# Q of all batches transposed by DMA, an opening ordered along its longest path, and split folds in a fused sorted-attention, Fourier-mix and MLP kernel

## The chip, the cores and the metric

The kernel runs on one core of one Trainium2 chip. The metric is the device time in microseconds (us), start to end. Executions of one kernel scatter here by about 2%, so small differences are judged only from ratios of fast runs of the same rounds, with their 95% intervals. A run is called slow when it took over 1.5% longer than the fastest run of the same kernel.

Five engines work side by side: TensorE multiplies matrices, VectorE and ScalarE work through their elements, GpSimd does small operations and issues loads, and SyncE issues transfers only. Each issues its transfers in order, as a queue; all queues are carried by 16 DMA engines. A transfer has landed when its completion is signalled. A point is one per cent of the time of the kernel before.

## The reference

Inputs are q, k, v (4 batches, 8 heads, 768 rows, 64 columns), a sorting matrix per batch and head, and two MLP weights. Cut to what matters:

```python
P = sort_net                                  # five Sinkhorn steps on 8x8 matrices
for _ in range(5):
    P = exp(P - max); P = P / rowsum; P = P / colsum
k_sorted = einsum('bhij,bhjcd->bhicd', P, k_blocks)      # v_sorted likewise
attn = softmax(q_blocks @ k_sorted_blocks^T / 8) @ v_sorted_blocks
x = attn, heads side by side                             # (4, 768, 512)
u = x + real(fft(fft(x, axis=1), axis=2))
un = (u - mean(u)) / sqrt(var(u) + 1e-6)
out = u + relu(un @ w_ch1) @ w_ch2                       # w: 512x2048, 2048x512
```

## The kernel before

The program makes its own schedule. Every operation is an object with a cost per engine, what it reads and writes, and a priority; a list scheduler written in Python puts the operations in order on each engine. Hardware then runs each engine's list strictly in order.

Q must stand with the head dimension on partitions before the scores. For batches 2 and 3 (`QB`) the DMA transposes it; for 0 and 1 a copy regroups it, TensorE transposes it, and another copy brings it back.

```python
QB = (2, 3)
def load_qk(nm, b, hf, prio):
    src = {"k": k, "q": q}[nm]
    if nm == "q" and b in QB:                 # natural layout: one load per head, 128-byte runs
        for h in range(4):
            load(kq[:, slot[nm, b, hf], :].rearrange(...)[:, h // 2, h % 2], src[b, 4 * hf + h]..., ...)
        return
    load(kq[:, slot[nm, b, hf], :]..., ...)   # one large load of four heads
# in kqt(b, hp):
if b in QB:
    P.add({"SP": (1.4, 3.4)}, lambda _: nc.sync.dma_start_transpose(qt.ap..., kq[:, slot["q", b, hf], 768 * hl:768 * hl + 768]), ...)
    return
for r in range(6):
    nc.tensor.matmul(p16[:, 128 * r:128 * r + 128], qr.ap[:, r], idh, is_transpose=True)
# ... copied back to qt by ScalarE or VectorE
```

The weights w1 and w2, K, Q and V are loaded from GpSimd's queue. The sync queue carries the DMA transposes and, for each batch, three small copies that put the rows of the Fourier mix's correction in place (`rb<-rr`).

```python
for dst, src in ((rb[0:32, :], rr[o:o + 32, 0, :]), (rb[32:64, :], ...), (rb[64:96, :], ...)):
    P.add({"SP": (0.1, 2.3)}, lambda _, dst=dst, src=src: nc.sync.dma_start(dst, src), ...)
# dft1: two adds over all 512 columns fold the six row blocks
for n in range(2):
    V.tensor_tensor(pmt[:, 3 * n:3 * n + 3, 0:DM], rt.ap[:, 0:3, :], rt.ap[:, 3:6, :], op=add if n == 0 else subtract)
```

The softmax here doesn't subtract the row's maximum and nothing guards it: scores larger than these inputs give would overflow.

## Time and profile before

| | before |
|---|---|
| time, median of 3 runs (range) | 299.42 us (298.74 to 299.74) |
| the profiled run | 300.78 us, a slow run |
| its first product with w1, the first layer of the MLP | 76.06 us |
| w1 / w2 / V of batch 1 in flight (counted from the trace's DMA records) | 30.6–41.6 / 40.4–51.9 / 50.6–59.2 us |

Lines of the page and the views stand in the prediction. Three habits help to read them. A digit row is the span in 40 slices of 7.5 us, each digit the busy tenths. A busy TensorE is not a full one, so work is counted as matmuls times their closest spacing. And an average over the span hides the regimes: this kernel loses nearly all its time before the first normalised rows reach the MLP.

The only profile of the kernel before is of a slow run, and the prediction reads it without saying so. A fast one of nearly the same program came later: z2 below (295.71 us) has the same order of instructions on TensorE, VectorE, ScalarE and GpSimd, and one unread DMA transpose more. Its first w1 product comes at 72.6 us. Most of the difference arises early: in the slow profile the trace's first record of TensorE's full clock starts at 36.0 us, in z2's at 23.6 us. (The page's clock row shows 9s before that as well, where it has no record.) The mix of batch 0's V, first in the slow profile, then in z2 (duration in ns, first and last start in us):

```profile
L638 PE MATMUL bank<-bdv,vbn x64: 219/219/311, 30.6 to 40.2; 128*128 128x128 f16 x63, 128*96 128x128 f16 x1
L638 PE MATMUL bank<-bdv,vbn x64: 217/219/219, 29.1 to 36.1; 128*128 128x128 f16 x63, 128*96 128x128 f16 x1
```

Where an opening is compared below, z2 stands for the kernel before.

### The profile page before, as it was taken

What the parts mean: (1) busy time and instruction counts of PE and PEld (TensorE: products, weight loads), DVE (VectorE), ACT (ScalarE), POOL (GpSimd) and SP (SyncE); (2) the same over time, 40 slices, a digit from 0 to 9 for tenths busy, and PEclk for the clock granted to TensorE, in tenths of its full rate; (3) what the DMA queues carried; (4) which work ended last, traced back from release to release, by engine and by line L of the source; (5) the groups of instructions that cost most, each with busy time, mean ns of one, the idle gap of its engine ahead of it and who ended that gap; (6) DMA issues with size and microseconds to landing.
All of it is one profiled execution on the core that took longest, in us unless ns stands there. A gap on an engine that the chain in (4) does not pass through costs nothing.

```text
span 299.0 us, 5829 instructions
## 1 busy us (share of the span) xinstructions
PE 271.8 (91%) x2332; PEld 166.4 (56%) x2332; DVE 178.3 (60%) x395; ACT 153.3 (51%) x307; POOL 55.1 (18%) x91
## 2 busy tenths in 40 slices
PE   0499988884999999899999999999999999999994
PEld 0266976763556656555556645545645645645641
DVE  4797589999699999786249954314605315312001
ACT  2575579862647797468237703613721631641710
POOL 8964212012800036030002000200200010010000
PEclk9999999996699999999999999999999999999999
DMA  7999999980920249825010210031021121121002
GB/s 116 218 286 216 216 206 213 203 111 15 67 17 2 58 98 162 150 13 107 35 71 15 55 70 35 20 105 38 15 53 70 37 53 70 37 54 70 37 0 105
DMA packets 43025, 26.32 MB, mean 88 GB/s; under 512 B 29834, under 2 KB 38552, under 8 KB 42996
## 3 DMA queue, kind: packets, MB, share of 16 engines
q0 software_dynamic: 22576, 15.16, 33.3%
q1 hardware_dynamic: 20422, 10.78, 12.4%
q8 instruction: 18, 0.29, 0.4%
q14 instruction: 9, 0.07, 0.1%
HBM read 28.95 MB, written 6.29 MB: 118 GB/s over the span
## 4 chain that ended last, share of the span: by engine, by line
PE 72%; DVE 16%; DMA 4%; ACT 2%; issue 2%; POOL 2%; DVEq 0%; ACTq 0%; POOLq 0%
PE bank L1112 28%; PE bank L1091 25%; PE bank L635 3%; DVE rt L905 2%; DMA kq<-in_q_dram 2%; PE bank L1005 2%; PE bank L952 2%; PE bank L851 2%; PE bank L891 2%; DMA out_dram<-u 2%; PE bank L638 2%; DVE pmt L919 2%; PE bank L797 2%; DVE u L1020 1%; PE bank L1012 1%
## 5 line engine op out<-in xcount | busy, mean ns | idle before, releaser
L1103 ACT ACTIVATE hr<-bank 128x384 f16<-128x384 f32 x111 | 54.1, 490 | 79.9 <-PE bank L1091 79.7
L1091 PE MATMUL bank<-ut,w1sb 128*128 128x384 f16 x512 | 93.4, 331 | 0.7 <-DVE hr L1100 0.7
L1112 PE MATMUL bank<-w2sb,hr 128*128 128x512 f16 x384 | 89.0, 379 | 0.0
L1091 PEld LDWEIGHTS <-w1sb 128*128 128x128 f16 x512 | 49.5, 99 | 36.1 <-issue 3.0
L1112 PEld LDWEIGHTS <-hr 128*128 128x128 f16 x384 | 36.5, 98 | 40.6 <-issue 0.2
L1120 DVE TENSOR_TENSOR u<-bank,u 128x512 f32<-128x512 f32 x24 | 16.6, 690 | 51.5 <-PE bank L1112 51.0
L1020 DVE SCALAR_TENSOR_TENSOR u<-rt,bank 128x512 f32<-128x512 f16 x24 | 16.1, 678 | 35.6 <-PE bank L1012 29.7
L860 ACT ACTIVATE ex<-bank 96x384 f32<-96x384 f32 x64 | 27.9, 485 | 8.3 <-PE bank L851 6.5
L1033 POOL TENSOR_SCALAR mv<-mv 128x3 f32<-128x3 f32 x8 | 2.6, 320 | 141.8 <-DVE mv L1028 139.6
L1052 ACT ACTIVATE un<-u,nm,ny 128x512 f16<-128x512 f32 x14 | 11.4, 811 | 14.6 <-POOL nm L1042 9.0
L395 POOL DMA_DIRECT2D kq<-in_q_dram x20 | 17.7, 905 | 4.2 <-ACT qr L571 1.9
L891 PE MATMUL bank<-vsf,eb 97*128 97x65 f16 x384 | 15.8, 195 | 2.7 <-DVE u L1020 1.3
L905 DVE TENSOR_TENSOR rt<-bank,rz 128x384 f16<-128x384 f32 x32 | 17.3, 550 | 0.4
L874 ACT ACTIVATE eb<-ex,negone 96x384 f16<-96x384 f32 x29 | 17.5, 614 | 0.2
L891 PEld LDWEIGHTS <-eb 97*128 97x128 f16 x384 | 14.3, 98 | 4.8 <-issue 2.9
L571 ACT CAST vsf<-bank 96x512 f16<-96x512 f32 x19 | 13.9, 790 | 4.3 <-PE bank L638 3.4
L1026 DVE BATCH_NORM_STATS2 st<-u 128x6 f32<-128x512 f32 x24 | 15.9, 682 | 0.2
L395 POOL DMA_DIRECT2D kq<-in_k_dram x8 | 6.5, 808 | 49.9 <-issue 27.8
L826 PE MATMUL bank<-pack,qr 128*128 128x128 f16 x48 | 5.3, 264 | 11.0 <-ACT qr L571 10.2
L635 PE MATMUL bank<-bdv,vcx 128*128 128x128 f16 (+1 forms) x128 | 14.2, 238 | 1.1 <-ACT bdv L571 1.1
L872 DVE TENSOR_SCALAR eb<-ex 96x384 f16<-96x384 f32 x35 | 13.1, 377 | 1.7 <-ACT ex L860 1.6
L797 PE MATMUL bank<-bdk,kq 128*64 128x128 f16 x192 | 11.8, 247 | 1.5 <-DVE u L1020 1.0
(114 smaller groups left out, 337.8 us busy)
## 6 DMA issues: line engine op xcount, KB each, us to landing
out_dram<-u SPq DMA_DIRECT2D x24, 256.0 KB, 2.0
kq<-in_k_dram POOLq DMA_DIRECT2D x8, 384.0 KB, 9.2
w1sb<-in_moe_w_ch_dram POOLq DMA_DIRECT2D x4, 512.0 KB, 15.2
w2sb<-in_moe_w_ch_dram POOLq DMA_DIRECT2D x4, 512.0 KB, 19.0
kq<-in_q_dram POOLq DMA_DIRECT2D x4, 384.0 KB, 11.3
hr<-in_v_dram POOLq DMA_DIRECT2D x2, 768.0 KB, 11.5
kq<-in_v_dram POOLq DMA_DIRECT2D x2, 768.0 KB, 21.3
kq<-in_q_dram POOLq DMA_DIRECT2D x16, 96.0 KB, 6.0
```

Of the source, the lines that this page charges most:

```text
L395: return P.add({eng: c}, lambda _: e.dma_start(dst, src), r=r, w=w, prio=prio, nbytes=nbytes, tag="load", after=after)
L635: nc.tensor.matmul(o, vcx[:, 96 * d:96 * d + m], bd, start=True, stop=(t == 1))
L797: nc.tensor.matmul(ps.ap[64 * h2:64 * h2 + 64, 128 * r3:128 * r3 + 128], k16[:, 2 * hl + h2, 3 * half + r3, :], bdk[:, 2 * hp + h2].rearra ...
L860: nc.scalar.activation(ex.ap, pss[h2].ap[0:96, 0:384], AF.Exp, scale=SCALE),
L874: nc.scalar.activation(ed, src, AF.Identity, bias=negone[0:96])
L891: nc.tensor.matmul(po.ap[:, 65 * T:65 * T + 65], eb.ap[:, e0:e0 + 128], vsf[:, vi:vi + 65], start=(n == 0), stop=(n == 1), skip_group_chec ...
L905: P.add({"DVE": (0.45, 0.56)}, lambda _: V.tensor_tensor(rt.ap[:, :, D * h:D * h + D], po3()[:, :, 0:D], rz.ap[:, :, None].broadcast_to([1 ...
L1020: V.scalar_tensor_tensor(u.ap.rearrange("p (m n) -> p m n", n=2), rt.ap[:, T, :].rearrange("p (m n) -> p m n", n=2), RSC, ps.ap.rearrange( ...
L1091: nc.tensor.matmul(ps.ap[:, 0:GT], w1sb[:, c, 128 * fc:128 * fc + 128], ut.ap[:, c, :], start=(c == 0), stop=(c == 3))
L1103: nc.scalar.activation(hr[g][:, fc, :], ps.ap[:, 0:GT], AF.Relu)
L1112: nc.tensor.matmul(ps.ap, hr[g][:, fc, 128 * tt:128 * tt + 128], w2sb[:, fc, :], start=(fc == 0), stop=(fc == 15))
L1120: V.tensor_tensor(u.ap, ps.ap, u.ap, op=ALU.add),
```

## The change

Its intent is to shorten that opening: take the Q transposes and their copies off TensorE, ScalarE and VectorE, and let the scheduler follow the longest path to the first normalised rows. The diff, cut to its core (left out: bookkeeping of tiles, other scratch buffers for the correction rows, and two constants of the scheduler's model of loads):

```diff
-QB = (2, 3)
+LOOK = {"DVE": 0.8, "ACT": 0.8, "PE": 0.8}
+QB = (0, 1, 2, 3)
...
+    def aim(self, goal):                # priority = length of the longest path to the goal
+        tail = {goal: 0.0}
+        for o in reversed(self.ops):
+            if o in tail:
+                for p in o.preds:
+                    tail[p] = max(tail.get(p, 0.0), tail[o] + best(o))
+        for o, t in tail.items():
+            o.crit = True
+            if o.nbytes == 0:
+                o.prio = -1000.0 - t
...
+                        if not o.crit and e in LOOK:   # don't start an operation off the path if one on
+                            ...                        # the path gets ready within 0.8 of its cost
...
-    many("qr", 2, [128, 6, 128], F16)
-    many("qt", 3, [128, S], F16)
+    many("qt", 5, [128, S], F16)
...
-        for n in range(2):
-            P.add({"DVE": (0.86, 0.95)}, ...tensor_tensor(pmt[:, 3 * n:3 * n + 3, 0:DM], ...
+        for c in range(2):
+            for n in range(2):
+                cc = slice(256 * c, 256 * c + 256)
+                P.add({"DVE": (0.44, 0.55)}, ...tensor_tensor(pmt[:, 3 * n:3 * n + 3, cc], ...
...
-            if b > 0:
+            if b + g > 0:               # second row group of batch 0 by DMA transpose too
...
-    at(-30.0, (dft1, (0,)), (dft2, (0, 0)), (dft2, (0, 1)))
+    at(-30.0, (dft1, (0,)))
+    goal.append(dft2(0, 0))
+    at(-29.0, (dft2, (0, 1)))
```

More of the change, by code (lines that the diff above doesn't have):

```diff
@@ L101 @@
     __slots__ = ("n", "costs", "fn", "preds", "succs", "left", "ready", "prio",
-                 "vts", "fresh", "nbytes", "end", "start", "eng", "tag")
+                 "vts", "fresh", "nbytes", "end", "start", "eng", "tag",
+                 "crit")
 class Buf:
@@ L116 @@
 class Plan:
-    HBM = 330.0
+    HBM = 400.0
     DLAT = 2.2
@@ L134, in add @@
         o.n = len(self.ops)
+        o.crit = False
+        o.end = o.start = None
         o.costs, o.fn, o.nbytes, o.tag = costs, fn, nbytes, tag
@@ L166, in add, with best @@
         return o
+    def aim(self, goal):
+        def best(o):
+            return min(c[1] for c in o.costs.values()) + self.XL
+        tail = {goal: 0.0}
[7 more added lines that the diff above has]
+                o.prio = -1000.0 - t
     def schedule(self):
@@ L202, in slot_time, with soonest @@
             return (None if short else t), short
+        crits = [o for o in self.ops if o.crit]
+        def soonest(c, e):
+            if e not in c.costs:
+                return None
+            for p in c.preds:
+                if p.start is None:
+                    if p.left or len(p.costs) > 1:
+                        return None
+                    x, = p.costs
+                    return max(free[x], p.ready[x]) + p.costs[x][1] + self.XL
+            return None
         while todo:
             pick = None
+            want = {}
+            near = [c for c in crits if c.start is None and c.left == 1]
+            for e in free:
+                for o in avail[e]:
+                    if o.fresh and o.ready[e] <= free[e] + 0.3:
+                        for p in slot_time(o, ())[1]:
+                            want[p] = min(want.get(p, o.prio), o.prio)
             for e in free:
@@ L209, in schedule @@
                 soon = None
-                held = set()
                 for o in sorted(avail[e], key=lambda o: (o.prio, o.n)):
@@ L213, in schedule @@
                     if o.fresh:
-                        st, short = slot_time(o, held)
-                        if o.ready[e] <= t + 0.3:
-                            held |= short
+                        st, short = slot_time(
+                            o, [p for p in want if want[p] < o.prio])
                         if st is None:
@@ L220, in schedule @@
                     if s <= t + 1e-9:
+                        if not o.crit and e in LOOK:
+                            x = t + LOOK[e] * o.costs[e][0]
+                            n = [c.ready[e] for c in avail[e] if c.crit
+                                 and t < c.ready[e] < x]
+                            n += [y for y in (soonest(c, e) for c in near)
+                                  if y is not None and t < y < x]
+                            if n:
+                                n = min(n)
+                                if soon is None or n < soon:
+                                    soon = n
+                                continue
                         cand = o
@@ L408, in qk16, with kqk @@
             "p (h r d) -> p h r d", h=4, r=6)
+    def kqk(n):
+        return [("kq", n, h) for h in range(4)]
     def load_qk(nm, b, hf, prio):
@@ L417, in load_qk @@
                     src[b, 4 * hf + h].rearrange("(r p) d -> p r d", r=6),
-                    196608, [("kq", slot[nm, b, hf])], prio + 0.01 * h)
+                    260000, [("kq", slot[nm, b, hf], h)], prio + 0.01 * h)
             return
@@ L422, in load_qk @@
                  "h (p r) d -> p h (r d)", r=6), 786432,
-             [("kq", slot[nm, b, hf])], prio)
+             kqk(slot[nm, b, hf]), prio)
     def hk(g):
@@ L432, in load_v @@
             [("nat", t, hf)] + (hk(0)[8 * hf:8 * hf + 8] if t == 0 else
-                                [("kq", 2 * hf), ("kq", 2 * hf + 1)]), prio)
+                                kqk(2 * hf) + kqk(2 * hf + 1)), prio)
     def load_w1(c, prio):
@@ L476 @@
     for n, nm in enumerate(("pw", "pack", "vrow", "erow", "rrow")):
-        load_c(nm, -500.0 + n, "SP")
-    load_qk("k", 0, 0, -500.0)
-    load_qk("q", 0, 0, -499.0)
-    load_v(0, 0, -498.0)
-    load_v(0, 1, -497.0)
-    load_qk("k", 0, 1, -496.0)
-    load_qk("q", 0, 1, -495.0)
-    load_c("dtab", -494.0)
-    load_c("lt", -493.0)
+        load_c(nm, -5000.0 + n, "SP")
+    load_qk("k", 0, 0, -5000.0)
+    load_qk("q", 0, 0, -4999.0)
+    load_v(0, 0, -4998.0)
+    load_v(0, 1, -4997.0)
+    load_qk("k", 0, 1, -4996.0)
+    load_qk("q", 0, 1, -4995.0)
+    load_c("dtab", -4994.0)
+    load_c("lt", -4993.0)
     load_c("cs", 19.0)
@@ L581, in v_path @@
         psm = Buf("pm", "pf") if t else Buf("pm")
-        stage = [("kq", n) for n in range(4)] if t else hk(0)
+        stage = [i for n in range(4) for i in kqk(n)] if t else hk(0)
         for hf in range(2):
@@ L673, in a_path @@
         pa = Buf("pf")
-        bd_, bp_ = Buf("qt"), Buf("qt")
+        bd_, bp_ = Buf("un"), Buf("un")
         P.add(pe(0.4), lambda _: nc.tensor.matmul(
@@ L709, in a_path @@
         px, pr = Buf("pf"), Buf("pf")
-        hi, hi2 = Buf("qt"), Buf("qt")
+        hi, hi2 = Buf("yr"), Buf("ex")
         def f(_):
@@ L731, in a_path @@
               r=[pr], w=[hi], tag="rhi")
-        P.add(evac(512), lambda e: copy(e, hi2.ap[0:64, 0:512],
+        P.add(evac(512), lambda e: copy(e, hi2.ap[0:64, 0:256].bitcast(F16),
                                         px.ap[0:64]),
@@ L748, in a_path @@
             rr[0:64, 1, :].rearrange("p (n m) -> p n m", n=2),
-            hi2.ap[0:64, 0:512].rearrange("p (m n) -> p n m", n=2),
+            hi2.ap[0:64, 0:256].bitcast(F16).rearrange(
+                "p (m n) -> p n m", n=2),
             nlo[0:64], px.ap[0:64].rearrange("p (m n) -> p n m", n=2),
@@ L755, in a_rows @@
         o = 32 * (b % 2)
-        for dst, src in ((rb[0:32, :], rr[o:o + 32, 0, :]),
-                         (rb[32:64, :], rr[64 + o:96 + o, 0, :]),
-                         (rb[64:96, :], rr[o:o + 32, 1, :])):
+        for n, (dst, src) in enumerate((
+                (rb[0:32, :], rr[o:o + 32, 0, :]),
+                (rb[32:64, :], rr[64 + o:96 + o, 0, :]),
+                (rb[64:96, :], rr[o:o + 32, 1, :]))):
             P.add({"SP": (0.1, 2.3)}, lambda _, dst=dst, src=src:
                   nc.sync.dma_start(dst, src),
-                  r=[("rr", i) for i in (0, 1, 2, 3, 256)], w=["rb"],
+                  r=[("rr", i) for i in (0, 1, 2, 3, 256)], w=[("rb", n)],
                   tag="arow")
@@ L782, in q_copy @@
             e, qr.ap.rearrange("p r (h d) -> p r h d", h=2), src),
-            r=[("kq", slot["q", b, hf])], w=[qr], tag="qcp",
+            r=kqk(slot["q", b, hf])[2 * hl:2 * hl + 2], w=[qr], tag="qcp",
             after=[exps[-1]] if first else [])
@@ L801, in f @@
                             bdk[:, 2 * hp + h2].rearrange("p i c -> p (i c)"))
-            P.add(pe(0.22), f, r=[("kq", slot["k", b, hf]),
+            P.add(pe(0.22), f, r=kqk(slot["k", b, hf]) + [
                                   ("bdk", hp // 2)],
@@ L817, in kqt @@
                 kq[:, slot["q", b, hf], 768 * hl:768 * hl + 768]),
-                r=[("kq", slot["q", b, hf])], w=[qt], tag="qX")
+                r=kqk(slot["q", b, hf])[2 * hl:2 * hl + 2], w=[qt],
+                tag="qX")
             return
@@ L896, in av @@
         P.add(pe(0.5), f, r=[(eb, 0), (eb, 1), "erow", "vrow", "vsz"]
-              + [("vsb", n) for n in range(16)], w=[po], tag="av")
+              + [("vsb", n) for n in range(16)], w=[po, (rts[b], "a", h)],
+              tag="av")
         rz = Buf("rz")
@@ L917, in dft1 @@
         hs = [(rt, h) for h in range(H)]
-        for n in range(2):
-            P.add({"DVE": (0.86, 0.95)}, lambda _, n=n: V.tensor_tensor(
-                pmt[:, 3 * n:3 * n + 3, 0:DM], rt.ap[:, 0:3, :],
-                rt.ap[:, 3:6, :], op=ALU.add if n == 0 else ALU.subtract),
-                r=hs, w=[("pm", n), ("fq", 0), ("fq", 1)],
-                tag="pmt")
+        for c in range(2):
+            for n in range(2):
+                cc = slice(256 * c, 256 * c + 256)
+                P.add({"DVE": (0.44, 0.55)}, lambda _, n=n, cc=cc:
+                      V.tensor_tensor(
+                          pmt[:, 3 * n:3 * n + 3, cc], rt.ap[:, 0:3, cc],
+                          rt.ap[:, 3:6, cc],
+                          op=ALU.add if n == 0 else ALU.subtract),
+                      r=hs[4 * c:4 * c + 4],
+                      w=[("pm", n, c), ("fq", 0), ("fq", 1)], tag="pmt")
         P.add({"ACT": (0.17, 0.22)},
@@ L926, in dft1 @@
                   pmt[:, :, DM:DM + 1], pmt[:, :, 0:1]),
-              r=[("pm", 0), ("pm", 1)], w=["pm2"], tag="pmc")
-        pms = [("pm", 0), ("pm", 1), "pm2"]
+              r=[("pm", 0, 0), ("pm", 1, 0)], w=["pm2"], tag="pmc")
+        pms = [("pm", n, c) for n in range(2) for c in range(2)] + ["pm2"]
         P.add({"DVE": (0.88, 0.97)}, lambda _: V.tensor_tensor(
@@ L1016, in dft2 @@
                   r=[y4[c][g] for c in range(4)]
-                  + ["rb", "rrow", "lt", "lt96", "lt96a", "lt96b", "dtab"],
+                  + [("rb", n) for n in range(3)] + ["rrow", "lt", "lt96", "lt96a", "lt96b", "dtab"],
                   w=[ps, u], tag="dft2")
@@ L1081, in dft2 @@
                   r=[pt], w=[(ut, tt, 1)], tag="utev")
+        return P.ops[-1]
     def mlp(b, g, pr_pe, pr_v):
@@ L1134, in attn @@
             av(b, h)
+    goal = []
     def at(p, *fns):
@@ L1169 @@
     with tc.manual_schedule():
+        P.aim(goal[0])
         for o in P.schedule():
```

## The prediction

> **What bounds the kernel now.** I read the page first: the busy shares, then the 40 slices.
>
> ```profile
> PE 271.8 (91%) x2332; PEld 166.4 (56%) x2332; DVE 178.3 (60%) x395; ACT 153.3 (51%) x307; POOL 55.1 (18%) x91
> ...
> PE   0499988884999999899999999999999999999994
> ...
> DVE  4797589999699999786249954314605315312001
> ACT  2575579862647797468237703613721631641710
> ...
> PEclk9999999996699999999999999999999999999999
> DMA  7999999980920249825010210031021121121002
> ```
>
> The kernel has two regimes. From slice 11 on TensorE is full and VectorE thins out; before that, VectorE and the DMA queues are the full rows. The 91% hides this, because the end of a matmul is modelled. So I next took the chain that ended last and looked at how far apart matmuls start.
>
> ```profile
> 76.06 3.95 PE bank L1091 x12
> ...
> 101.37 0.86 PE bank L1112 x4
> ...
> 276.19 8.45 PE bank L1091 x52
> 284.64 10.37 PE bank L1112 x48
> ```
>
> Packed, a first-layer matmul (L1091) takes 8.45/52 = 0.1625 us and a second-layer one (L1112) 10.37/48 = 0.216 us. The first twelve take 0.329 us each: half clock. In the same way I took 0.040 us for an attention-times-V matmul, 0.0285 for a score, 0.0445 for a K mix, 0.056 for 128 columns, 0.083 for 193, 0.109 for 256. Count times spacing gives TensorE's real work: 39.5 us before 76.06, 22.8 to 101.3, 30.2 to 134.4, 159.0 to 295.1. The stretches last 76.1, 25.2, 33.1 and 160.7 us, so the time without work is **36.5, 2.4, 2.9 and 1.7 us**. After the last matmul 3.9 us remain. The kernel loses its time in the opening, before the first normalised rows reach the MLP. The view by stretch says who is busy there:
>
> ```profile
> 0.00:76.06 76.06, 54.75 (x703) 42.77 (x704) 62.72 (x161) 47.34 (x91) 30.91 (x52) 0.96 0.97 177
> 76.06:101.20 25.14, 25.08 (x221) 16.27 (x221) 22.59 (x46) 15.42 (x32) 5.45 (x6) 0.91 0.42 35
> ```
>
> The columns are length, then PE, PEld, DVE, ACT, POOL busy, clock, DMA share, GB/s. VectorE is busy 85.3 of 101.2 us. Its 15.9 us of idle time lie mainly before 40 us: waits for the sort matrix, for the V load, for the V mix. From 40 to 70 us it is idle 1.2 us in all. Until about 101 us, when the last ReLU of the first MLP is done and L1112 can start, I therefore count **VectorE** time; after that, TensorE work.
>
> **What the Trainium skill says.** "TensorE: Matmul & The Clock Gate", Part 1, says the array runs at half rate until it has been busy for a window. The trace agrees: 0.329 against 0.1625 us, and a row of 6s in the clock. "DMA: Bandwidth & Descriptors", DMA Transpose (X-bar), restricts the transpose to 2-byte types and to the sync and scalar queues; here it is fp16 on the sync queue, 1.21 us to issue and 2.7 us to land. The same page, Issuing engines are not separate DMA queues, says that all queues share 16 engines; the DMA row (9s up to slice 7) shows there is little room for more in the opening. "Perfetto Trace Analysis", Identifying the Most-Contended Engine, calls matmul busy time a poor measure: 271.8 us busy against 254 us of work here.
>
> **The change, part by part.**
>
> *Q by DMA for batches 0 and 1.* Removed (a group of the page, then the form list of the copy helper's line: count, least/median/most ns, first and last start):
>
> ```profile
> L826 PE MATMUL bank<-pack,qr 128*128 128x128 f16 x48 | 5.3, 264 | 11.0 <-ACT qr L571 10.2 <-DVE rt L905 0.3 <-DVE rr L747 0.3
> L571 ACT COPY qr<-kq x5: 813/825/844, 9.3 to 55.2; 128x768 f16<-128x768 f16 x5
> L571 ACT COPY qt<-bank x5: 798/802/811, 12.0 to 59.3; 128x768 f16<-128x768 f16 x5
> L571 DVE COPY qt<-bank x3: 944/947/958, 11.1 to 45.0; 128x768 f16<-128x768 f16 x3
> L571 DVE COPY qr<-kq x3: 332/347/349, 26.5 to 46.6; 128x768 f16<-128x768 f16 x3
> ```
>
> TensorE: 48 x 0.056 = 2.7 us of work. ScalarE: 5 x 0.825 + 5 x 0.802 = 8.1 us. VectorE: 3 x 0.947 + 3 x 0.347 = 3.9 us. One of those VectorE copies sits at 11.08 us inside the sort iterations and holds the chain for 0.9 us. Added: 8 transposes on the sync queue, and Q loads cut in four:
>
> ```profile
> kq<-in_q_dram POOLq DMA_DIRECT2D x4, 384.0 KB, 11.3
> ...
> kq<-in_q_dram POOLq DMA_DIRECT2D x16, 96.0 KB, 6.0
> ...
> qt<-kq SPq DMA_TRANSPOSE x8, 2.7
> ```
>
> A 96 KB load moves 768 packets of 128 bytes. In the backlog near 118 us about 1,170 such packets start per us, so four take 2.6 us; the one load of 384 KB that they replace takes 1.9 us. Issuing four costs GpSimd 4 x 0.85 = 3.4 us. The four half batches thus put the weight loads back by some 3 us (estimate): w1, landed near 42 us before, lands near 45, long before its use. V lands at most 1 us later.
>
> *Second row group of batch 0 by DMA.* 12 x 0.056 = 0.7 us less on TensorE, and three copies of 0.42 to 0.58 us less. Total TensorE work: 254.4 - 2.7 - 0.7 = 251.0 us.
>
> *Order.* I read the built program's instruction order. The V path now comes before most of batch 0's attention; the first row group is folded and normalised first; only 120 instead of 168 attention-times-V matmuls, 96 instead of 128 scores and 90 instead of 96 K mixes stand before the first L1091. That is 1.9 + 0.9 + 0.3 = 3.1 us of work that moves behind it. Split folds cost nothing much: eight adds of 0.95 us become sixteen of about 0.49 us.
>
> *First MLP start.* Before, the V mix ran from 30.5 to 41 us. Now it can start when V has landed (17.5 us), its sum is done (20.5), reduced (21.5), scaled and masked: 24 to 25 us, ending near 34. VectorE's instructions from there to the third row tile, by their durations, are some 31 us; 34 + 31 plus 1 to 3 us of waits gives the first L1091 at **66 to 68 us** instead of 76.06.
>
> *The end.* The start itself is not the gain, since VectorE must still finish batch 1. I summed all VectorE instructions up to the last ReLU of the first MLP, each with its mean duration: 94.5 us before, 90.6 after. Scaled to the busy time of 85.3 us (instructions overlap a little) that is 3.6 us less. TensorE work still to do at that point: 1.1 us less (3.4 us is removed for good, but in the new order 2.3 us less has been done by then). So the gain is 3.6 + 1.1 = 4.7 us, plus whatever VectorE saves of its 15.9 us of idle time. I count 11.4 us of idle time to the end of the V mix (34 less 22.6 us of work) against 13 before, none lost to half-clock ReLUs at 76 to 80 us, but some for the look-ahead's deliberate waits: about 13.5 us. That saves 2.4 us: gain 7.1 us, total **292.3 us**.
>
> **Rivals.**
> (a) *VectorE is the bound and only its order changes.* If the look-ahead holds VectorE back as much as the new order saves, idle stays at 16 us, and 4.7 us is all: 294.7. For it: between 40 and 70 us VectorE had no idle time to give.
> (b) *The early start pays in full.* If TensorE fills as soon as the MLP starts, 9 us less 3.1 deferred plus 3.4 removed gives 9.3: 290. Against it: between the first L1091 and the last of those ReLUs some 28 us of VectorE work stand beside only 25 us of TensorE work in the new order.
> (c) *The DMA queue takes the place of the removed copies.* If small Q packets and transposes hold V up by 3 us, the whole opening moves: 295 to 296. For it: DMA is at 9 in slices 1 to 7. Against it: V is issued after one half batch of Q, whose data used to stand before it as well.
> (d) *Nothing reaches the end*, as TensorE is full later anyway. Against it: that regime has only 7 us of gaps and simply starts earlier.
>
> **Range and chances.** Between (a), my sum and (b) lie 290 to 295 us. The VectorE idle figure is good to 4 us, the sums to 2. Predicted 292.5, range 288 to 298. The 2% line is at 293.4, just above the prediction: faster 0.55, same 0.43, slower 0.02.
>
> **What would show it.** First L1091 at 64 to 69 us and first L1112 at 93 to 98; TensorE work before the first L1091 near 33 us; VectorE idle up to the first L1112 near 13.5 us; no L571 copies of Q, 16 transposes qt<-kq; w1 landed before 50 us; gaps after the first L1112 still under 6 us. The prediction is wrong if V lands after 19 us, if the first normalised rows wait for a transpose or for GpSimd (its chain now has a 0.8 us load issue inside), or if TensorE shows more than 6 us of gaps between the first L1091 and the first L1112.

## The result, and the profile after

| | before | after |
|---|---|---|
| median of 4 runs of the same rounds (range) | 299.08 us (294.53 to 299.74) | 325.88 us (324.57 to 335.75; the last is a slow run) |
| ratio of fast runs, 95% interval | 1 | 1.0971 (1.0765 to 1.1178) |
| first w1 product / first w2 product | 76.06 / 101.37 us (slow profile; z2: 72.6 / 96.8) | 95.36 / 123.5 us |
| w1 / w2 / V of batch 1 in flight | 30.6–41.6 / 40.4–51.9 / 50.6–59.2 | 41.4–59.3 / 53.4–74.5 / 69.7–81.9 us |
| matmuls | 2332 | 2272 |

A ratio is the mean time of one kernel's fast runs over the mean of the other's fast runs of the same rounds, so it is not quite the ratio of the medians quoted. The changed kernel is 9.7% slower; all runs were correct.

The page of the changed kernel, slices as before:

```profile
PE   0379976001979999987999999999999999999995
...
DVE  5797999000789999977925795431461431431002
...
PEclk9995995655679999998999999999999999999999
DMA  9999999999949200599402020203011203012002
```

A slice is 8.1 us here. TensorE and VectorE now stand still together in the eighth to tenth slice (56 to 80 us), while the DMA engines are full up to the eleventh. Before, no slice of the opening after the first was empty on either engine. From the thirteenth slice on TensorE is as full as it was. The busy times of the opening and of the first MLP stretch, in the columns that the prediction explains:

```profile
0.00:95.36 95.36, 49.24 (x569) 36.42 (x570) 60.20 (x144) 35.38 (x69) 44.99 (x68) 0.77 1.33 160
95.36:123.50 28.14, 27.66 (x335) 18.12 (x336) 27.25 (x67) 25.35 (x56) 0.86 (x1) 0.99 0.37 58
```

In the opening VectorE does slightly less than before (60.20 against 62.72 us) but in 19 us more of time; it is not the bound any more. The second stretch is as dense as its counterpart before. So most of the loss lies before the first w1 product: 22.7 of the 28.9 us between the spans of this profile (322.8 us) and of z2 (293.9 us). The other 6 us lie after it: about 2 us of work that was moved there, and TensorE's time without work, 10.7 us against 6.6.

TensorE's two longest waits, and the steps from 23 us on of the chain of work that ended last (start, length, step):

```profile
PE bank L1068 <- DMA kq<-in_q_dram: 23.0, 1, 23.0
PE bank L634 <- DMA hr<-in_v_dram: 13.2, 1, 13.2
```
```profile
23.24 4.14 POOL kq L440 x5
27.38 12.45 DMA kq<-in_k_dram
40.11 19.44 DMA w1sb<-in_moe_w_ch_dram
59.84 19.53 DMA kq<-in_q_dram
79.43 0.59 PE bank L1068
```

The chain is made of DMA for 52 us on end. L1068 is the product that needs the correction rows `rb`; the second transform and everything after it waits for them. The view names a Q load as its releaser, because that came last by the semaphore records; the product does not read Q. What it does read is `rb`, so I looked at that tile and at the sync queue (start, length, queue, line, operation):

```profile
8.45 53.53 SPq L865 DMA_TRANSPOSE qt<-kq  x8
62.04 26.18 SPq L810 DMA_DIRECT2D rb<-rr  x6
```
```profile
L810 SPq DMA_DIRECT2D rb<-rr x6: 507/586/803, 62.0 to 87.7; - x6
...
DMA to landing us min/median/max: 2.1/15.5/16.0
```

Eight Q transposes occupy the sync queue until 62 us; for 24.0 us of this the queue waits for the Q loads that they read, and for 16.5 us for TensorE, so their own slowness is not all of the hold. The row copies stand behind them (in e4 below, where they don't, they go out at 48.1 us), and then take up to 16 us to land; before they were issued at 56.44 us and took at most 4.9. In the list of DMA issues (operation, count, KB each, median us from issue to landing) the transposes themselves have changed:

```profile
kq<-in_q_dram POOLq DMA_DIRECT2D x32, 96.0 KB, 11.2
...
qt<-kq SPq DMA_TRANSPOSE x16, 8.8
```

Before, a transpose took 2.7 us to land, and a small Q load 6.0. The 8.8 us are the median of all sixteen; of the eight in the opening, the five whose landing is recorded took 9.6 to 16.5 us. The number of issues was expected, the times were not.

### The profile page after: what moved, and what is told of

It is laid out like the page before. It is cut to its first block, busy times and chain, and to the rows that moved or that the text cites.

```text
span 322.8 us, 5741 instructions
## 1 busy us (share of the span) xinstructions
PE 269.0 (83%) x2272; PEld 162.1 (50%) x2272; DVE 180.4 (56%) x398; ACT 144.9 (45%) x293; POOL 63.6 (20%) x103
## 4 chain that ended last, share of the span: by engine, by line
PE 65%; DMA 22%; POOL 6%; DVE 5%; issue 1%; ACT 0%; POOLq 0%; DVEq 0%
PE bank L1169 26%; PE bank L1148 24%; DMA kq<-in_q_dram 6%; DMA w1sb<-in_moe_w_ch_dram 6%; DMA kq<-in_k_dram 4%; DMA out_dram<-u 3%; PE bank L1061 3%; POOL kq L440 3%; PE bank L942 3%; DMA hr<-in_v_dram 2%; PE bank L1008 2%; PE bank L847 2%; PE bank L1068 2%; POOL eb L493 2%; PE bank L902 1%; PE bank L683 1%
## 5 line engine op out<-in xcount | busy, mean ns | idle before, releaser
L1148 PE MATMUL bank<-ut,w1sb 128*128 128x384 f16 x512 | 94.5, 329 | 0.0
L1169 PE MATMUL bank<-w2sb,hr 128*128 128x512 f16 x384 | 88.0, 379 | 0.0
L1160 ACT ACTIVATE hr<-bank 128x384 f16<-128x384 f32 x105 | 51.4, 490 | 79.2 <-PE bank L1148 78.7
L1148 PEld LDWEIGHTS <-w1sb 128*128 128x128 f16 x512 | 48.1, 98 | 33.9 <-issue 1.3
L1169 PEld LDWEIGHTS <-hr 128*128 128x128 f16 x384 | 37.2, 98 | 41.5
L1177 DVE TENSOR_TENSOR u<-bank,u 128x512 f32<-128x512 f32 x24 | 16.6, 691 | 59.9 <-PE bank L1169 59.6
L1076 DVE SCALAR_TENSOR_TENSOR u<-rt,bank 128x512 f32<-128x512 f16 x24 | 16.3, 685 | 58.4 <-PE bank L1068 52.0
L440 POOL DMA_DIRECT2D kq<-in_q_dram x32 | 26.6, 855 | 26.8 <-DMA w2sb<-in_moe_w_ch_dram 12.5
L1068 PE MATMUL bank<-rb,vcx 97*128 97x512 f16 x24 | 10.4, 432 | 23.0 <-DMA kq<-in_q_dram 23.0
L619 ACT CAST ks<-bank 128x384 f16<-128x384 f32 x21 | 9.2, 481 | 33.3 <-PE bank L847 33.2
L942 PE MATMUL bank<-vsf,eb 97*128 97x65 f16 x384 | 17.2, 199 | 1.6 <-DVE rt L957 1.1
L942 PEld LDWEIGHTS <-eb 97*128 97x128 f16 x384 | 15.4, 101 | 4.2 <-issue 1.4
L634 PE MATMUL bank<-hr,pack 128*128 128x512 f16 x12 | 5.5, 626 | 13.2 <-DMA hr<-in_v_dram 13.2
L847 PE MATMUL bank<-bdk,kq 128*64 128x128 f16 x192 | 11.7, 236 | 4.1 <-DVE u L1076 1.7
```

The lines of the kernel that those rows point to most:

```text
L440: return P.add({eng: c}, lambda _: e.dma_start(dst, src), r=r, w=w, prio=prio, nbytes=nbytes, tag="load", after=after)
L619: (nc.scalar.copy if e == "ACT" else V.tensor_copy)(dst, src)
L847: nc.tensor.matmul(ps.ap[64 * h2:64 * h2 + 64, 128 * r3:128 * r3 + 128], k16[:, 2 * hl + h2, 3 * half + r3, :], bdk[:, 2 * hp + h2].rearra ...
L942: nc.tensor.matmul(po.ap[:, 65 * T:65 * T + 65], eb.ap[:, e0:e0 + 128], vsf[:, vi:vi + 65], start=(n == 0), stop=(n == 1), skip_group_chec ...
L1068: nc.tensor.matmul(ps.ap, lt[:, 128 * T:128 * T + 128], rb, start=False, stop=True, skip_group_check=True)
L1148: nc.tensor.matmul(ps.ap[:, 0:GT], w1sb[:, c, 128 * fc:128 * fc + 128], ut.ap[:, c, :], start=(c == 0), stop=(c == 3))
```

## The experiments

Fifteen kernels ran, all correct. Times are medians; each ratio is to the kernel before, which ran beside it (its medians were 297.2 to 298.5 us). x3 and x4 have two runs each, e1 and z2 twenty, z3 twelve, the others four.

| run | what it is | us | ratio (95% interval) |
|---|---|---|---|
| e1_q_pe | the change, but Q of batches 0 and 1 by TensorE | 298.20 | 1.0063 (1.0029–1.0096) |
| e2_q0_dma | the change, but Q of batch 1 by TensorE | 307.33 | 1.0386 (1.0308–1.0464) |
| e3_before_qdma | before, all Q by DMA | 321.26 | 1.0817 (1.0697–1.0937) |
| e4_rows_act | the change, row copies from ScalarE's queue | 325.62 | 1.1010 (1.0931–1.1090) |
| x1_small_pe | the change with its small Q loads, transposed by TensorE | 304.37 | 1.0269 (1.0209–1.0329) |
| x2_big_dma | the change with large Q loads, then a copy, then DMA transposes | 332.97 | 1.1194 (1.1055–1.1332) |
| x3_rows_act_q2_late | e4 with batch 2's Q loads later | 317.76 | 1.0719 (1.0608–1.0831) |
| x4_w_after_t | the change, weights loaded after batch 1's transposes | 318.87 | 1.0757 (1.0622–1.0891) |
| y1_before_junk4 | before + four unread DMA transposes at 28 us | 309.11 | 1.0407 (1.0333–1.0482) |
| y4_before_junk4_late | before + the same four at 72 us | 299.93 | 1.0058 (0.9941–1.0175) |
| z2_before_junk1 | before + one unread transpose at 29 us | 298.60 | 0.9980 (0.9940–1.0020) |
| z3_before_rows_act | before, row copies from ScalarE's queue | 297.81 | 1.0037 (0.9998–1.0076) |
| z1_junk4_rows_act | z3 + the four of y1 | 303.44 | 1.0188 (1.0113–1.0264) |
| y3_b1_dma_free | the change, only batch 0's Q by TensorE | 306.40 | 1.0300 (1.0194–1.0405) |
| y2_b1_dma_gated | y3, batch 1's transposes held until V has landed | 305.10 | 1.0272 (1.0185–1.0358) |

### Which part of the change costs the time

**e1_q_pe** keeps the order, the look-ahead, the split fold and the second row group by DMA, and takes back Q of batches 0 and 1.

```diff
-QB = (0, 1, 2, 3)
+QB = (2, 3)
-    many("qt", 5, [128, S], F16)
+    many("qr", 1, [128, 6, 128], F16)
+    many("qt", 4, [128, S], F16)
```

> The changed kernel with Q of batches 0 and 1 back on TensorE (buffers for the copies: one instead of two, four transposed instead of five); order, look-ahead and split fold kept. Theory 1 (the rows copy rb<-rr stands on the sync queue behind batch 1's Q transposes, which crawl beside the weight loads): the 23 us hole before the first L1068 is gone, 290 to 297 us. Rival 2 (too much DMA work in the opening, whichever queue): also 290 to 297. Rival 3 (the new order or the look-ahead is the loss): stays above 315 us.

Measured: 298.2 us, 0.6% over before. (The limit of 1.5% calls 9 of the 23 runs of the kernel before slow, and 1 of 20 of e1; with all runs counted the means differ by 0.1%.) So the loss is in the Q part, and the rest of the change gains nothing. Where its gain went can be read in part. The first w1 product came at 73.19 us: 2.9 us earlier than in the slow profile of the kernel before, but no earlier than the 72.6 us of z2. Counted alike in these two fast profiles, TensorE's time without work up to 110 us is 34.3 us in e1 and 36.5 in z2, a gain of 2.2 us. Then more was given back: from 110 to 200 us it is 8.2 us against 2.6. The largest single wait there:

```profile
PE bank L903 <- DVE u L1077: 4.0, 1, 4.0
```

TensorE stands 4 us for VectorE's residual add. Work that was moved off the path to the first rows is still VectorE's work; that it came due in the next stage fits this wait, but no run tests it.

**e2_q0_dma** puts only batch 0's Q on the DMA way; **e3_before_qdma** puts all Q there in the old order.

```diff
-QB = (0, 1, 2, 3)
+QB = (0, 2, 3)        # e2, in the changed kernel;  e3: QB = (0, 1, 2, 3) in the kernel before
```

> Only batch 0's Q by DMA, batch 1's on TensorE. Theory 1: batch 0's transposes are done by 30 us, before the weight packets, so nothing holds the rows copy: no hole, 290 to 298 us. Rival 2 (total DMA work): half of the extra DMA work is left, so about half of the loss, 308 to 314 us. Rival 3: above 315 us.

> The kernel before with only Q of batches 0 and 1 by DMA; old order, no look-ahead. Theory 1: the sync queue has the same order (eight transposes, then the rows), so a hole of 15 to 25 us before the first dft2 row matmul and 312 to 325 us. Rival 2: the same. Rival 3: at most 302 us.

Measured: 307.3 and 321.3 us (e3's profile is of a slow run, so no time is read from it). e2 misses theory 1. Batch 0's half costs some 3 points, and batch 1's nearly 6 more on top of it. Alone, batch 1's half costs 2.4 (y3 below, less e1), so the two together cost more than their sum. The old order suffers as well: the loss does not need the new order. e3's time lies in the range of theory 1, but not for its reason: in e3's program the sync queue issues the three row copies before the eight transposes, not behind them.

**x1_small_pe** and **x2_big_dma** separate the two things that "Q by DMA" brings: small packets and transposes. In x1 the four loads per half batch stay, but TensorE reads them and transposes; no copy is needed. In x2 one large load comes back, a copy regroups it, and the DMA transposes the copy.

```diff
# x1
+QP = (0, 1)           # natural-layout loads as changed, but six TensorE transposes straight from kq
# x2
-QB = (0, 1, 2, 3)
+QB = (2, 3)           # loads of 0 and 1 large again, qr <- kq copied
+    nc.sync.dma_start_transpose(qt.ap..., qr.ap...)
```

> The changed kernel, Q of batches 0 and 1 still loaded as four small transfers of 128-byte packets, but turned on TensorE straight from the loaded tile: no DMA transpose before batch 2. Theory A (the DMA transposes in flight beside the loads are what slows the loads, packet for packet): w1 is in by 46 us, no slow weight packets, 293 to 301 us. Theory B (the small packets and their many issues on GpSimd are the load that is too much): w1 stays after 55 us and the time at 312 us or more.

> The reverse: Q of batches 0 and 1 loaded in one large transfer per half batch, regrouped by ScalarE or VectorE as before, then turned by DMA transpose (scores read the tile with a stride). Theory A: weight packets again alternate with 256-byte transpose packets and some take over 0.6 us; w1 after 52 us; 312 to 326 us. Theory B: no small packets, so near 298 us as with Q on TensorE.

Measured: 304.4 and 333.0 us. x1 lies between both theories, and w1 landed at 49.8 us, not by 46. Small packets alone cost 2.7% less e1's 0.6%, so about 2 points or 6 us (a working). The transposes are the larger part: from x1's 2.7% to 9.7% for the full change. x2, without the small packets, is no better than the change (its profile is of a slow run, and it brings copies back as well, so I take from it only that large loads don't cure the loss).

### Taking the new waits away, one at a time

**e4_rows_act** frees the row copies from the sync queue.

```diff
-            P.add({"SP": (0.1, 2.3)}, lambda _, dst=dst, src=src: nc.sync.dma_start(dst, src),
+            P.add({"ACT": (0.1, 2.3)}, lambda _, dst=dst, src=src: nc.scalar.dma_start(dst, src),
```

> The changed kernel with the rows copies issued from ScalarE's queue instead of the sync queue; all transposes and loads as they are. Theory 1: the rows land within 3 us, the first L1068 runs near 57 us instead of 79; then batch 1's scores wait for its last Q transposes (landed near 72 us before), so part of the loss is left: 300 to 312 us. Rival 2 (DMA work itself is too much): the rows copies crawl on the other queue too and the time stays above 318 us. Rival 3: above 315 us.

Measured: 325.6 us, no gain at all, against theory 1. The wait went as intended: L1068 now started at 58.3 us in place of 79.4. Another took its place. TensorE's longest wait, and the chain that ended last:

```profile
PE bank L1127 <- DVE u L1076: 24.3, 1, 24.3
```
```profile
57.52 30.17 DMA kq<-in_v_dram
87.69 0.28 issue
87.97 0.82 POOL kq L440
89.20 0.89 POOL ny L1092
```

GpSimd computes a few operations of the normalisation, but its list is in order, and load issues that wait for room or for a buffer stood before them. The statistics were held until V had come in.

**x3_rows_act_q2_late** removes that as well: the next batch's Q loads are issued only after these statistics. **x4_w_after_t** instead makes the weight loads wait, in the order of issue, until batch 1's transposes are planned to be over.

```diff
# x3, on top of e4
-        load_qk("q", 2, hf, 62.5 + hf)
+        load_qk("q", 2, hf, 62.5 + hf, after=[lnop[0, 0]])
# x4, on the changed kernel
+        for o in wops:                  # the eight loads of w1 and w2
+            o.preds.update(x for x in P.ops if x.tag == "qX" and ...)   # batch 1's four transposes
```

> e4_rows_act with batch 2's Q loads issued only after the first rows' statistics on GpSimd. Theory A with two held queues (the loss reaches the end because the sync queue holds the rows copy and GpSimd's queue holds the statistics, both behind transfers): with both freed the first L1148 starts by 72 us instead of 97 and the time is 298 to 308 us though the loads stay slow. If the slow loads act by themselves (w1, w2 or V of batch 1 late): above 316 us.

> The changed kernel with the w1 and w2 loads held until batch 1's four Q transposes have landed. Theory A: those transposes land by 50 us instead of 72, the rows copy is issued by 52 us instead of 62 to 79, no weight packet takes over 0.6 us; weights in by 75 us; the statistics on GpSimd still stand behind loads, so 303 to 314 us. Theory B: no gain, above 320 us.

Measured: 317.8 and 318.9 us. In x3 the first w1 product came at 73.7 us, 21.6 us earlier than in the changed kernel and within about 1 us of z2, and still the time is 7.2% over the kernel before: V of batch 1 was in only at 85.6 us, and batch 1's attention, which could have filled the time between the MLP's matmuls, was missing. In x4 the transposes were done by 54 us, but w1 landed at 78.9. Each repair gains some 8 us at most and shows the next wait. That suggests the DMA traffic itself, not one of the waits; the next runs measure a part of it.

### The cost of a transpose by itself

These runs take the kernel before and add only transposes whose results nobody reads. On TensorE and GpSimd the order of instructions is unchanged in y1 and y4.

```diff
# y1: batch 1's Q, as soon as it has landed, into a spare part of a buffer that is written later anyway
+    junk = hr[1].rearrange("p a b -> p (a b)")[:, 3456:4224]
+    for n in range(4):                  # z2: range(1)
+        P.add({"SP": (1.4, 3.4)}, lambda _, n=n: nc.sync.dma_start_transpose(
+            junk.rearrange("p (r s) -> p r s", r=6),
+            kq[:, slot["q", 1, n // 2], 768 * (n % 2):768 * (n % 2) + 768]), ...)
# y4: the same four of batch 1's V, after V has landed and the row copies have gone out
```

> The kernel before with nothing changed but four more DMA transposes, whose results nobody reads: batch 1's four natural-layout Q blocks, as soon as they have landed (about 32 us), into a spare part of the second hidden buffer; every engine other than the sync queue has the order of before. No small Q packets are added. Theory (transposes in flight make the ordinary loads slow): w1 lands at 45 to 50 us (41.6 before), w2 at 55 to 60 (51.9), V of batch 1 at 62 to 68 (59.2), slow weight packets of 0.6 to 2 us appear, and the time is 301 to 306. Rival (only the small Q packets and their issues cost, transposes fit beside loads): the loads land within 1 us of before and the time is within 0.5% of before.

> The same four unread transposes in the kernel before, but of batch 1's V after it has landed and after the rows have gone out, so after about 60 us, when the weights and V are in. Theory: the cost of a transpose is what it does to the loads beside it, so here it is nothing: loads as before, time within 0.5% of before (296.5 to 299.5). Rival (a transpose costs time by itself on the queue or the engines wherever it is): 301 to 306 as for the early ones.

Measured: 309.1 us early, 299.9 late: four transposes that nobody needs cost 4.1%, or 12 us, at 28 us, and nothing that can be resolved at 72 us (the interval reaches from -0.6% to +1.8%; that they were issued near 72 us is from the profile of a slow run, of which nothing else is used). So the cost belongs to the moment. The profile of y1, the sync queue with its wait for its own transposes (us in total, times, longest), TensorE's longest wait and the list of issues:

```profile
28.29 39.07 SPq L1149 DMA_TRANSPOSE hr<-kq  x4
67.45 12.99 SPq L760 DMA_DIRECT2D rb<-rr  x6
```
```profile
SPq L1149 <- DMA hr<-kq: 34.0, 3, 16.0
```
```profile
PE bank L1012 <- DMA rb<-rr: 14.4, 1, 14.4
```
```profile
hr<-kq SPq DMA_TRANSPOSE x4, 10.2
```

My expectation had only a part of it. w1, expected at 45 to 50 us, was not slowed: it landed at 42.4 (42.3 in z3, a fast profile without these transposes). w2 and V were late, as expected: 55.7 (52.5) and 63.9 us (60.1). What I had not expected is that the **transposes** crawl, 39 us for four, and that the row copies behind them were issued at 67.45 in place of 56.44 (52.3 in z2). A part of the 39 us is made by the experiment: all four write the same place, so the program lets each start only when the one before has landed (34.0 us of waiting). In the changed kernel the transposes write to five buffers in turn, and the queue waits for their loads and for TensorE instead.

The single records of the DMA engines show the pace. Each transpose is 768 records of 256 bytes, over 16 engines. In y1 from 32 to 34 us, 97 records of w1 (4096 bytes, 322 ns each) started and 99 records of the transpose (29 ns each): as many of one as of the other. The records don't name their engine, so that they alternate one by one is inferred. z3, without transposes, starts 103 of w1 in the same 2 us. Alone, near 100 us in the kernel before, some 610 transpose records started per us; beside w1 some 50. An estimate from these: an engine starts a record of w1 every 2 x 16 / 97 = 0.33 us, so the 768 / 16 = 48 turns of a transpose beside w1 take 15.8 us. **z2_before_junk1** measures just this.

> The kernel before with one early unread transpose in place of four, rows on the sync queue. Theory A: it is issued near 28 us, its packets are in flight for about 10 us, done long before the rows at 56 us, so the time is within 0.5% of before. Theory B: a quarter of the four's cost, 2 to 3.5 us (0.7 to 1.2%). If transposes cost no more beside loads than alone, and only a queue of several is slow, its packets are done in 3 us.

```profile
hr<-kq SPq DMA_TRANSPOSE x1, 16.1
```

A single transpose beside w1 takes 16.1 us to land, six times the 2.7 us of the kernel before. That the estimate is so close is in part luck: its records are in flight for 11.7 us (33.1 to 44.8), faster at the end as w1 runs out at 43.3 us, and some 4 us pass before the first of them, for a reason that no run shows. And it costs nothing: 0.998 of before, although V landed at 61.8 us, 1.7 us later than in z3. It was over at 45 us, before the rows went out at 52.3. So not the slowness as such costs time, but what has to stand behind or wait for it.

**z3_before_rows_act** and **z1_junk4_rows_act** split y1's 12 us. z3 is e4's edit in the kernel before; z1 is z3 with y1's four transposes.

> The kernel before with the small row copies (rb<-rr) issued from ScalarE's queue in place of the sync queue; no transposes added. A control for the next run. Both theories: within 1.5% of before (295 to 303), first w1 product at 74 to 80 us; the rows land near 59 us as before.

> The control plus the four early unread transposes. Theory A (the cost of a transpose beside loads is that it takes about 10 us and holds the sync queue, so the row copies behind it come late): with the rows on another queue the four cost at most 1% against the control (0 to 3 us), the 14.4 us wait of TensorE for rb is gone, and the first w1 product comes within 3 us of the control. Theory B (the cost is the slowed weight and V loads): the time is 9 to 13 us over the control, as the same four cost over the kernel before, and TensorE waits for another thing as long.

Measured: 297.8 us and 303.4 us. With the rows on another queue the same four transposes cost 1.9 - 0.4 = 1.5 points instead of 4.1. So of y1's cost about 2.6 points, near 8 us, are the hold on the sync queue, and some 1.5 remain (differences of ratios, good to about a point); neither theory as I wrote it (at most 1%, or all of it) is met. TensorE's wait for `rb` fell from 14.4 to 2.8 us (1.7 in z3). What makes the remaining 1.5 points I could not read off: V landed 2.2 us later than in z3, but the one profile of z1 also lost some 4 us before 50 us to a lower TensorE clock (0.77 against 1.00 from 30 to 40 us). The fast profiles of y1, z2 and z3 did not have this; the slow one of the kernel before, whose full clock is first recorded at 36.0 us, did. That part stays open. And the hold is not what costs the changed kernel its time: there the same move of the rows (e4) gained nothing.

### Transposes off batch 0, and held back

**y3_b1_dma_free** gives batch 0's Q back to TensorE in the changed kernel; **y2_b1_dma_gated** adds a tiny copy on the sync queue that reads batch 1's V, so that batch 1's transposes start after all big loads have landed.

```diff
-QB = (0, 1, 2, 3)
+QB = (1, 2, 3)
# y2 also:
+    gate = P.add({"SP": (0.1, 2.3)}, lambda _: nc.sync.dma_start(gate_t, nat[1][0:1, 3064:3080]),
+        r=[("nat", 1, 0), ("nat", 1, 1)], after=<the three row copies of batch 0>, ...)
+    # batch 1's four transposes come after the gate
```

> The changed kernel with batch 0's Q by TensorE and copies, batches 1 to 3 by DMA, batch 1's transposes as soon as their Q lands (beside w1 and w2). Theory: 305 to 312, w1 landing at 48 us or later with slow packets. Rival (the harm came from batch 0's transposes alone): 298 to 302.

> The kernel of the run before this, same loads, same transposes, but batch 1's transposes stand on the sync queue behind a tiny copy that reads batch 1's V, so none of them is in flight while weights and V come in. Theory: w1 lands at 43 to 46 us without slow packets, w2 by 58, V by 65; batch 1's scores begin late (after 66 us) and the time is 298 to 304, at least 3 us under the ungated one. Rival (the small packets are the cost): the same time as the ungated one within 1%. If batch 1's scores are needed before 66 us, the gate itself opens a hole on TensorE at 60 to 68 us and the gain is given back.

Measured: 306.4 and 305.1 us. In y3 the time is as expected, but w1 landed at 43.6 us: not late. The gate did what it was for. In y3 TensorE waits for `rb` again, 9.8 us at a stretch; in y2 that wait is gone, w2 landed at 53.6 us in place of 57.0, and the first w1 product came at **66.25 us**, the earliest of all runs and inside the predicted 66 to 68. Yet the time is the same within the intervals, as the rival said, and a miss of the 3 us that I expected at least. Batch 1's scores came late instead: TensorE's time without work was 9.4 us from 42 to 60 us and 17.3 us from 70 to 150 us (7.0 and 8.2 in e1). Here the early start of the MLP gained nothing; that it lacked other work to put between its matmuls fits these gaps.

No version beat the kernel before, so none is offered in its place.

## Why the prediction was wrong

The prediction said 292.5 us; it was 325.9, outside the range on the far side.

**The step that failed is the cost of the added transposes.** The text put each at "1.21 us to issue and 2.7 us to land", read off the kernel before, where they are issued between 98 and 137 us, those with a recorded landing in slices in which the DMA row of the page shows 2, 4 and 5. In the changed kernel eight of them run between 8 and 75 us beside K, V and the weights, where they took 9.6 to 16.5 us as far as recorded, and one alone beside w1 takes 16.1 us (z2). The same paragraph then counted only their GpSimd issues and packets against the weights.

**"w1, landed near 42 us before, lands near 45"** failed with it: w1 landed at 59.3. Its loads started 10.8 us later, behind Q loads that now ended at 43.4 us in place of 31.7, and then took 18 us in place of 11. The first half is in line with x1, where small packets alone start w1 at 37.2 us. The second half is not the sharing described above, which hardly slows w1 (y1): in the changed kernel, from 40 to 44 us, w1's records took 1.44 us each on average instead of 0.32. Of the GpSimd queue's records of 1024 bytes and more, 126 took over twice the median of their size, 122 us of engine time in all, or 7.6 us of 16 engines. Kernels without transposes beside the loads have next to none of them (before, e1 and z3 none, x1 3); those with them have between 2 (e2) and 202 (e4). What makes them slow, and why so unevenly, is not settled.

**"V lands at most 1 us later"** was right for batch 0 (16.6 us after, 16.3 before). It was the wrong transfer to guard. V of batch 1 came 22.7 us later, and the row copies, which the prediction never followed, stood behind the transposes, with a hole of 23 us. That came close to one of its own signs of being wrong, "if the first normalised rows wait for a transpose". Closing this hole gained nothing by itself (e4), as GpSimd's statistics, another sign that it named, then waited as long.

**Rival (c), "the DMA queue takes the place of the removed copies", was the right rival**, with the evidence named (9s in the DMA row up to slice 7), but it was sized at 3 us through V alone. The cost of this term was taken from the wrong stretch, and so the range ended at 298.

**The removals were right.** 60 matmuls are gone (2332 to 2272), no Q copies are left, and VectorE is not the bound: it is busy 60.2 of the first 95.36 us. TensorE's work before the first w1 product is 33.8 us, near 33 as predicted. "Until about 101 us I count VectorE time" was thus true of the kernel before and not of the changed one, in which both engines idle together.

**The order's gain was over-counted too, though this is small beside the rest.** Without Q by DMA (e1) the first w1 product came at 73.2 us, not at 66 to 68, and the total was 0.6% over before. y2 reached 66.25 us and gained nothing. One reason lies in the profile that was read: in it, a slow one, the V mix starts its last matmul at 40.2 us. The prediction let the new order end the mix near 34 us, and counted this as a gain over 41. In the fast z2 the old order already starts the last one at 36.1 us, in e1 the new order at 34.6. Rival (d), that an early start doesn't reach the end because later work is still due, fits this part: the 2.2 us that e1 has over z2 by 110 us had become a loss of 3.4 by 200 us.

Two sums of the prediction are off as well, without weight for the result: its four stretches of TensorE work add up to 251.5 us, not 254.4, and 3.9 us scaled by 85.3/94.5 is 3.5 us, not 3.6.

The sum, from ratios to the kernel before: order and folds +0.6 points, small Q packets about +2, transposes in flight beside the loads about +7; together 9.7%. It holds for this order of steps only, as the halves of e2 and y3 don't add up. That the Q part costs the time is shown by taking it back; through which waits the 7 points arise is shown for a part only.

## What to carry to other kernels

Take the duration of a DMA from the stretch in which it will run: a transpose that landed in 2.7 us late in the kernel took 16 us beside a weight load, where as many of its small records started as of the load's large ones. Before putting slow transfers on a queue, list what stands behind them in the same queue: in y1 three row copies behind four transposes nobody needs made up about 2.6 of 4.1 points. Before trusting the profile that a prediction starts from, check whether its run was a slow one. And in this opening, with the DMA engines at 90% or more, the Q transposes were cheaper left on TensorE.

## What the Trainium skill lacked or had wrong

- "DMA: Bandwidth & Descriptors", Rules for kernel authors, says of order between queues that "A transpose next to ordinary DMAs needs nothing". All runs were correct, so that holds for the data. That rule has no word on time: four transposes beside ordinary loads took a median of 10.2 us each, one beside w1 16.1 us, against 2.7 us late in the kernel, and four unread ones cost 4.1% of the kernel (a part of it by writing one place in turn).
- The same page, Queues, rings and completion order, says that each engine takes turns between queues and drains a whole packet of some 9 to 17 descriptors before it switches. The counts here fit turns, 97 records of 4096 bytes to 99 of 256 bytes in 2 us; how many records a turn has can't be read from them. What a kernel writer needs is the consequence, that a transpose beside a load took 16.1 us instead of 2.7, and the page doesn't draw it.
- "VectorE: DVE Perf Modes", The three transpose paths, gives 1309 ns for a DMA transpose of 128x128. Here six such blocks in one instruction landed in 2.7 us late in the kernel, 0.45 us a block, and in 16.1 us beside w1, 2.7 us a block. One figure without the load beside it does not serve to choose the path.
- No page has the slow records: 4096-byte w1 records of 0.32 us that took 1.44 us on average over 4 us of the changed kernel.
- The same first page, Issuing engines are not separate DMA queues, is right that another issuing engine shares the same 16 engines, and says that it saves only issue time. Here it also freed what stood behind: with the row copies on ScalarE's queue the four transposes cost 1.5 points instead of 4.1. In the changed kernel it gained nothing (325.6 us).
